# Rests of 64 tokens in 512 B pieces by head pair, measured starts in the plan, and a last store in three parts

## The chip, the cores and the metric

One core of one Trainium2 chip. The metric is the device time of one execution in microseconds (us). All runs that are compared are of the state "fast", and each kernel was timed beside the kernel before on the same chip. A ratio is the mean time of one kernel's fast runs over that of the other's fast runs of the same rounds, so it is not quite the quotient of the medians that are also given. A ratio difference of 0.01 is about 2.5 us.

## The reference, cut to what matters

Two attentions in a row, then a feed-forward layer. With B, H, S, D = 8, 8, 576, 64 and 32 packed queries `p`:

```python
p_packed = sm_attn(p, k, v)                  # 32 x 64 per head
out = sm_attn(q, p_packed, p_packed)         # 576 x 64 per head
x = out.transpose(0, 2, 1, 3).reshape(4608, 512)
h = x @ w_in                                 # 512 x 2048
g = h * (1 / (1 + exp(-beta * h)))
return g @ w_out                             # 2048 x 512
```

All inputs are float32 in device memory: q, k, v are 9.4 MB each, w_in and w_out 4 MB each. The output is 9.4 MB.

## The kernel before: the parts that matter

A small planner inside the kernel simulates the engines with a cost for each task and emits every engine's instructions in the resulting order. Ranks with some 1100 hand-searched offsets decide between tasks that are ready. All loads and stores are issued by SyncE (SP), in that order; an engine never skips a waiting instruction.

S = 576 is 512 tokens that spread over 128 partitions, and a **rest** of 64 tokens. For each of q, k, v and each batch the rest (128 KB) is loaded by two DMAs of 64 partitions; each piece is one token of one head, 256 B:

```python
for g in range(2):
    nc.sync.dma_start(
        t[64 * g : 64 * g + 64, :].rearrange("p (h d) -> p h d", h=4),
        src[b, 4 * g : 4 * g + 4, SM:S, :].rearrange("h p d -> p h d"),
    )
```

When the planner has nothing for the tensor engine (PE) before its own 48 us, it emits a useless matmul, which keeps PE busy:

```python
if e == "PE" and now < WARM_UNTIL:
    self.filler()
    free[e] = now + 0.11
```

The last of the 18 output units is stored by one DMA of 512 KB after its last quarter is ready.

The softmax here doesn't subtract the row's maximum and nothing guards it: scores larger than these inputs give would overflow.

## Time and profile before

| | before |
|---|---|
| time, median of 3 (range) | 252.02 us (251.88 to 252.15) |
| span of the profiled run | 250.0 us |
| PE busy, fillers among its matmuls | 237.0 us, 211 |
| last filler, end of the last matmul | 43.4 us, 245.8 us |
| data moved from 2 to 48 us | 324 GB/s on average |
| granted PE clock | 1.00 throughout |

The prediction shows the page and the chain that these stand on.

### The profile page before, as it was taken

The page shows a single profiled execution, that of the slowest core. Times are in us where ns is not written, and L with a number is a line of the kernel's source. Part 1 is how long each engine was busy: PE and PEld are TensorE (multiplying, and loading weights), DVE is VectorE, ACT ScalarE, POOL GpSimd, SP SyncE. Part 2 cuts the span into 40 slices and gives each one's busy share as a digit, 9 for nine tenths or more (in the row PEclk, how much of TensorE's full clock was granted, in tenths as well). Part 3 has the DMA queues.
Part 4 walks back from the last instruction along what each step waited for, and adds up shares of the span by engine and source line. Part 5 has one row for each costly group of instructions (what it writes and reads, how often), then busy time and mean ns, then how long its engine had stood idle before and what let it go on. Part 6 is the DMA issues. An engine that isn't in the chain of part 4 may idle for free.

```text
span 250.0 us, 6818 instructions
## 1 busy us (share of the span) xinstructions
PE 237.0 (95%) x2852; PEld 191.1 (76%) x2852; DVE 174.1 (70%) x327; ACT 176.6 (71%) x312; POOL 71.0 (28%) x119
## 2 busy tenths in 40 slices
PE   4999879899999999999999999999999999999993
PEld 4997557356657987888688977897889878898882
DVE  7464778689679839953996778836983597546752
ACT  2276357697879896898889867987699868875200
POOL 4044341434660164046205932341360000000000
PEclk9999999999999999999999999999999999999999
DMA  6999999999999999999999699999937020111042
GB/s 187 312 276 328 343 333 368 335 332 228 256 277 219 305 264 198 281 259 291 203 271 263 194 254 244 262 232 292 244 121 178 3 89 3 62 62 47 3 146 106
DMA packets 73486, 54.18 MB, mean 217 GB/s; under 512 B 42080, under 2 KB 66672, under 8 KB 73456
## 3 DMA queue, kind: packets, MB, share of 16 engines
q1 hardware_dynamic: 73456, 53.76, 79.2%
q8 instruction: 22, 0.36, 0.6%
q14 instruction: 8, 0.07, 0.1%
HBM read 37.23 MB, written 9.44 MB: 187 GB/s over the span
## 4 chain that ended last, share of the span: by engine, by line
PE 82%; DMA 9%; DVE 3%; SPq 2%; POOL 1%; issue 1%; ACT 0%; POOLq 0%; DVEq 0%
PE o_ps L294 44%; PE h_ps L294 22%; DMA v<-in_v_dram 5%; DMA w_in<-in_moe_w_in_dram 4%; PE w_ps L294 4%; PE hr_ps L294 3%; PE warm_ps L294 2%; PE s_ps L294 2%; PE z_ps L294 2%; SPq L364 1%; PE pp_ps L294 1%; DVE identr L976 1%; POOL w_in_bf L1104 1%; DVE pT L1026 1%; DVE k_bf L394 0%
## 5 line engine op out<-in xcount | busy, mean ns | idle before, releaser
L748 ACT ACTIVATE g_main<-h_ps 128x512 bf16<-128x512 f32 x128 | 71.1, 595 | 31.3 <-PE h_ps L294 30.8
L294 PE MATMUL h_ps<-A2T,W_bf 128*128 128x256 bf16 x512 | 70.1, 273 | 0.5 <-ACT g_rem L770 0.2
L294 PEld LDWEIGHTS <-W_bf 128*128 128x128 bf16 x768 | 56.3, 98 | 14.5 <-issue 7.2
L294 PEld LDWEIGHTS <-g_main 128*128 128x128 bf16 x512 | 48.7, 98 | 10.9 <-issue 1.7
L709 DVE SCALAR_TENSOR_TENSOR W_bf<-w_ps,rz,beta_bc 128x512 bf16<-128x512 f32 x64 | 44.8, 745 | 7.4 <-PE w_ps L294 7.2
L294 PE MATMUL o_ps<-w_out_bf,g_main 128*128 128x256 bf16 (+1 forms) x288 | 46.6, 296 | 0.7 <-DVE w_out_bf L1120 0.7
L294 PEld LDWEIGHTS <-g_sums 128*128 128x128 bf16 x384 | 36.6, 98 | 5.7 <-issue 0.7
L882 DVE COPY o_sb<-o_ps 128x256 f32<-128x256 f32 x48 | 20.2, 422 | 28.1 <-PE o_ps L294 27.5
L309 ACT ACT_TABLE_LOAD x28 | 35.9, 1283 | 1.2 <-PEq L1200 0.7
L294 PE MATMUL o_ps<-w_mix,g_sums 128*128 128x256 bf16 x256 | 34.6, 273 | 0.0
L394 POOL CAST v_bf<-v 128x512 bf16<-128x512 f32 x26 | 18.1, 736 | 47.7 <-PE o_ps L294 22.5
L294 PE MATMUL o_ps<-w_mix,g_main 128*128 128x256 bf16 x224 | 31.4, 273 | 0.0
L880 DVE TENSOR_TENSOR o_sb<-o_sb,o_ps 128x256 f32<-128x256 f32 x48 | 20.1, 419 | 13.5 <-PE o_ps L294 13.0
L394 POOL CAST q_bf<-q 128x512 bf16<-128x512 f32 x26 | 16.7, 684 | 18.6 <-DMA q<-in_q_dram 13.1
L294 PE MATMUL warm_ps<-identr 128*128 128x128 bf16 x211 | 18.3, 239 | 3.7 <-DVE bones L980 3.7
L394 POOL CAST k_bf<-k 128x512 bf16<-128x512 f32 x26 | 15.4, 634 | 14.0 <-DMA k<-in_k_dram 4.1
L294 PEld LDWEIGHTS <-identr 128*128 128x128 bf16 x211 | 14.9, 109 | 5.1 <-DVE bones L980 3.7
L294 PE MATMUL o_ps<-w_out_bf,g_sums 128*128 128x256 bf16 x128 | 17.3, 273 | 0.0
L294 PE MATMUL w_ps<-w_in_bf,pp 64*32 64x512 bf16 x256 | 13.9, 386 | 1.2 <-DVE pp L584 1.0
L294 PEld LDWEIGHTS <-pp 64*32 64x32 bf16 x384 | 5.6, 88 | 11.8 <-issue 8.2
L651 DVE TENSOR_TENSOR A2T<-E2T,z_ps 128x512 bf16<-128x512 bf16 x16 | 10.8, 682 | 1.6 <-ACT z_ps L646 1.6
L882 ACT COPY o_sb<-o_ps 128x256 f32<-128x256 f32 x16 | 6.0, 373 | 7.9 <-PE o_ps L294 7.6
(91 smaller groups left out, 272.7 us busy)
## 6 DMA issues: line engine op xcount, KB each, us to landing
out_dram<-o_sb SPq DMA_DIRECT2D x16, 512.0 KB, 3.3
k<-in_k_dram SPq DMA_DIRECT2D x7, 1024.0 KB, 6.2
v<-in_v_dram SPq DMA_DIRECT2D x7, 1024.0 KB, 7.2
q<-in_q_dram SPq DMA_DIRECT2D x6, 1024.0 KB, 7.4
w_in<-in_moe_w_in_dram SPq DMA_DIRECT2D x4, 1024.0 KB, 9.8
w_out<-in_moe_w_out_dram SPq DMA_DIRECT2D x4, 1024.0 KB, 8.4
q<-in_q_dram SPq DMA_DIRECT2D x4, 512.0 KB, 8.2
k<-in_k_dram SPq DMA_DIRECT2D x2, 512.0 KB, 7.7
```

Of the source, the lines that this page charges most:

```text
L294: return self.nc.tensor.matmul(out, lhsT, rhs, start=start, stop=stop, tile_position=pos, skip_group_check=True)
L309: self.nc.scalar.preload_act_table_set(SETS[mode])
L364: nc.sync.dma_start(t[64 * g : 64 * g + 64, :].rearrange("p (h d) -> p h d", h=4), src[b, 4 * g : 4 * g + 4, SM:S, :].rearrange("h p d -> ...
L394: self.copy[engine](to[:, j : j + m], of[:, j : j + m])
L651: nc.vector.tensor_tensor(part(st[b, "A2"], i), part(st[b, "E2"], i), sums(i), ALU.mult)
L709: nc.vector.scalar_tensor_tensor(st[b, "W"][:, r, cols], st[b, "w", m][:], st[b, "rz1"][:, r : r + 1], self.beta_bc[:, cols], ALU.mult, AL ...
L748: nc.scalar.activation(st[b, v, "g"][:, :, f, :], st[b, "h", v, f][:].rearrange("p (q n) -> p q n", q=4), AF.Silu)
L880: nc.vector.tensor_tensor(o, o, ps, ALU.add)
L882: self.copy[engine](o, ps)
L976: nc.vector.tensor_copy(self.identr[:], self.ident32[:])
L1026: self.copy[engine](self.pT[h, :, 32 * r : 32 * r + 32].rearrange("p m (a s) -> p m a s", a=2)[..., 8 * i : 8 * i + 8], self.t["p_ps", i][ ...
L1104: self.copy[engine](self.w_in_bf[:, c, cols], self.t["w_in", n][:, c])
```

## The change

Its intent: pieces of 512 B for the rests of the first two batches, since the start of the kernel is bound by loads; a plan with measured durations and the real starts of the engines; a shorter last store. The core of the diff (cut: the new table of offsets, the new order of the first loads, the same layout carried through the products and sums, one constant, `pT`, set on another engine, beta spread in halves):

```diff
+LAST_UNIT = 17
+PAIRED = 2
+COST_US = {"g": 0.597, "h": 0.4376, ...}
+FREE_US = {"PE": 2.2, "ACT": 2.1, "DVE": 3.8, "POOL": 2.0}
-OFFSETS = {0: -15, 1: -1.5, ...}
+OFFSETS = {0: -63.2, 1: -4.8, ...}
 ...
             def rest(x=x, b=b, src=src):
+                if b < PAIRED:
+                    for h in range(2):
+                        nc.sync.dma_start(
+                            t[:, 128 * h : 128 * h + 128],
+                            src[b, h:H:2, SM:S, :].rearrange("c (p u) d -> c p (u d)", u=2),
+                        )
+                    return
 ...
         def exp1_rest():
+            if b < PAIRED:
+                for c in range(NC):
+                    rows = slice(32 * c, 32 * c + 32)
+                    nc.scalar.activation(...)       # four of 32x128 for two of 64x128
+                return
 ...
+        if number == LAST_UNIT:
+            for n, (qs, i) in enumerate((((0, 1), 4), ((3,), 5), ((2,), 6))):
+                self.task(("last", n), "SP", 0.5 * len(qs), lambda qs=qs: self.store_part(unit, qs), [taken[i]], -10)
```

A rest now lies as 4 head pairs x 32 token pairs on the 128 partitions. The two tokens of a pair are neighbours in memory, hence the 512 B.

## The prediction

> **What bounds the kernel now.** I read the page first, then the chain of waits in order of time, then tables by stretch for the first 60 us, then the timeline of the start and of the end.
>
> The page says that the tensor engine is the bound nearly everywhere, and where it is not:
>
> ```profile
> PE   4999879899999999999999999999999999999993
> DMA  6999999999999999999999699999937020111042
> PE 82%; DMA 9%; DVE 3%; SPq 2%; POOL 1%; issue 1%; ACT 0%; POOLq 0%; DVEq 0%
> L294 PE MATMUL warm_ps<-identr 128*128 128x128 bf16 x211 | 18.3, 239 | 3.7 <-DVE bones L980 3.7
> ```
>
> PE is at 9 in every slice from about 56 us to the end of the last but one. The last line warns that a busy PE is not always a useful one: 211 matmuls on `warm_ps` are fillers that the planner emits when PE has nothing to do before its clock of 48 us. Forty-five of them ran in 4.98 us (first lines of the chain below), 0.111 us each, so all take 211 x 0.111 = 23.4 us, the last one at 43.4 us. Of the 250.0 us span, PE does no useful work in these 23.4 us, in 3.7 us before its first instruction and in 4.2 us after its last one. The rest, about 219 us, is matmul work that the change does not shorten. So only three things can be won: fillers, head and tail.
>
> The chain of waits names what the fillers wait for, and what the tail is:
>
> ```profile
> 3.68 4.98 PE warm_ps L294 x45
> ...
> 20.03 11.77 DMA v<-in_v_dram
> ...
> 33.95 10.71 DMA w_in<-in_moe_w_in_dram
> 44.71 1.70 POOL w_in_bf L1104 x2
> ...
> 232.73 13.11 PE o_ps L294 x120
> ```
>
> Two loads, of v for batch 1 and of the third block of w_in, carry 22.5 us of the start. Neither is slow by itself: they stand in a queue. This table has, per stretch, the stretch, busy time of each engine, the granted clock (1.00 throughout), the DMA share and GB/s:
>
> ```profile
> 4.00:10.00 6.00, 6.00 (x58) 5.76 (x57) 3.03 (x10) 0.05 (x1) 0.00 (x0) 1.00 1.06 358
> 10.80:12.00 1.20, 1.20 (x19) 1.20 (x16) 1.20 (x3) 0.58 (x1) 0.00 (x0) 1.00 1.19 175
> 14.40:16.80 2.40, 2.40 (x34) 2.38 (x33) 1.29 (x2) 1.94 (x3) 0.66 (x2) 1.00 0.83 134
> 19.20:21.60 2.40, 2.13 (x53) 1.70 (x52) 1.11 (x3) 0.67 (x2) 0.82 (x1) 1.00 1.09 231
> 22.00:26.00 4.00, 3.74 (x54) 3.21 (x54) 2.56 (x5) 2.70 (x5) 2.34 (x5) 1.00 1.04 390
> 40.00:46.00 6.00, 5.28 (x62) 3.18 (x62) 4.78 (x10) 4.09 (x7) 1.33 (x3) 1.00 1.05 378
> ```
>
> All 16 DMA engines are busy, yet in three stretches they move half of what they otherwise move. Those are the rests: the casts that read them wait until 12.51 us (k, batch 0) and 16.37 us (v, batch 0), at the end of the first two dips. The start is therefore bound by the DMA stream, and the 256 B pieces of the rests are its worst part.
>
> **What the Trainium skill says.** (1) "DMA: Bandwidth & Descriptors", Specifications: transfers need at least 512 B to reach line rate; below that the engine reads, modifies and writes. The trace agrees: 134 to 231 GB/s in the dips, 358 beside them. (2) The same page, "Why small descriptors are slow": each packet has a fixed cost. It agrees here too: 358 GB/s where q, k, v come in 1 KB pieces, 378 to 390 where the weights' 2 KB pieces dominate. (3) The same page, "Why a DMA increments its semaphore by 16 and not by 1", how many engines: the count is the largest number up to 16 that divides the slowest dimension of both access patterns. The loads of before have 64 or 128 there, so 16 engines; the trace of before has no load with a smaller one to test it. (4) The same page, "Anatomy of one DMA", gives a fixed 2.0 us plus bytes over 436 GB/s for a DMA from GpSimd: an estimate of 3.2 us for 512 KB and 2.3 us for 128 KB. These stores come from SyncE, and the page has 3.3 and 2.4:
>
> ```profile
> out_dram<-o_sb SPq DMA_DIRECT2D x16, 512.0 KB, 3.3
> out_dram<-o_sb SPq DMA_DIRECT2D x8, 128.0 KB, 2.4
> ```
>
> **The change part by part.**
>
> *Rests.* Six rests (k, v, q of batches 0 and 1) of 128 KB. What one costs now: the dips lose (358-175) x 1.2 + (358-134) x 2.4 + (358-231) x 2.4 = 220 + 538 + 305 = 1063 KB against the plain rate, 2.97 us at 358 GB/s. They hold four rests (k0, v0, k1, q0 by issue order), so 0.74 us each, plus 0.37 us for the bytes themselves: 1.1 us of stream. With 512 packets over 16 engines, 32 each, that is 34 ns for a 256 B packet. A 1 KB packet takes 1024 B / (358/16 GB/s) = 46 ns, a 2 KB one about 85 ns at 384 GB/s; on that line a 512 B packet would take 26 ns (estimate).
>
> If the new loads use 16 engines: 256 packets, 16 each, 0.42 us: 0.68 us saved per rest, 4.1 us for six. But the source of the new load is a pattern of 4 heads x 32 pairs x 128 elements, and the heads do not merge with the pairs. Its slowest dimension is 4, and by (3) it would go on 4 engines: 64 packets on each of these, 1.7 us where 1.1 us was, so +0.6 us per rest and +3.5 us for six on the four engines that then finish every later bulk load last. The same part can win 4.1 us or lose 3.5 us of stream.
>
> How much of it reaches PE: the two loads of the chain stand behind five and six of the rests, but PE has useful work for about half of the first 44 us. I take 0.7 of the stream: -2.9 us or +2.5 us.
>
> *More work for the rests.* In each of two batches: two score matmuls of 256 columns instead of 128 (+0.12 us), two more for the sums and four more for the packed product (about 0.2 us at the spacing of the 10 sums in 0.39 us), and four exponentials where two stood at 0.27 us, +0.54 us on ACT. In batch 0 the ACT work is solid from the rest's exponential (17.90 us) to the end of the other two (19.57 us) and the packed product follows at once, so these 0.54 us can show; in batch 1 the v load ends later and hides them. All in all +0.4 us.
>
> *Last unit in three stores.* The last store of 512 KB is issued at 246.32 us, after the last take, and ends the program. Three of its quarters have been ready earlier: takes end every 0.87 us before. The last piece becomes 128 KB: 3.3 - 2.4 = 0.9 us saved, provided that the two earlier pieces, issued about 1 and 2 us ahead, do not hold the queue (issue takes 0.34 us).
>
> *The plan.* The scheduler gets measured durations and true starts of the engines, wider start-up spreading of beta, the memset of `pT` on DVE, and a new set of rank offsets. From the ranks in the diff I read that k of batch 0 now goes before q and the first two blocks of w_in stand behind the loads of batch 0. In the stretch where PE is solid nothing can come of it. In the start a better order makes useful work out of fillers; the order of before was searched too, so I take only -1.0 us, a judgement and not a count.
>
> *Sum.* With 16 engines: 252.0 - 2.9 + 0.4 - 0.9 - 1.0 = 247.6 us. With 4 engines and no recovery: 252.0 + 2.5 + 0.4 - 0.9 - 1.0 = 253.0 us.
>
> **The rivals.** *A, cheaper packets on 16 engines, 247.6 us.* For it: the dips are plain, and the scheduler's new cost for a rest (0.55 us for 0.8) says that its writer counts on a gain. Against: the slowest dimension. *B, four engines, but they catch up, about 250.5 us.* A single slice of the stream reaches 408 GB/s, 25.5 GB/s per engine against 22.4 in the 1 KB stretch; with twelve engines ahead of them the four may run at that, and then most of the +3.5 us is made up, and the plan and tail remain. *C, four engines that never catch up, 253.0 us:* if each engine's own rate is the limit, as the 46 and 85 ns suggest, every bulk load until the end of the start lands later and fillers or waits grow. *D, the rests are hidden anyway:* the gain is only plan and tail, 252.0 - 0.9 - 1.0 + 0.4 = 250.5 us, the same number as B by another road. A later bound (ACT 71%, DVE 70%) is unlikely to take over, as neither's share moves by more than half a per cent.
>
> **Range and chances.** I give A 45%, B and D together 35%, C 20%: 0.45 x 247.6 + 0.35 x 250.5 + 0.2 x 253.0 = 249.7, say 249.6 us. The range runs from a little under A to C: 246.8 to 252.8 us. Faster by over 2% means under 247.0 us, which needs A and a plan that gives more than I take: 16%. Slower by over 2% means above 257 us, beyond C: 3%. The rest, 81%, is within 2%.
>
> **What would show it.** Packets: six rests save 256 each (1536), the last store adds 256, so about 72,200 in place of 73,486, and about 39,000 under 512 B. The rate in the dips: gone under A; under B and C stretches with a low DMA share, as twelve engines stand idle, and rests that land later than 8 us after issue. Fillers: about 180 of 211 under A, as many or more under C. Tail: the end 3.3 us after the last matmul instead of 4.2 us. The stretch from the last filler to the last matmul should keep its length within 1 us of 202 us; if it grows, the error is in my claim that the change leaves the solid part alone. The prediction is wrong in kind if the start shrinks without a faster stream: then it is the order of loads that did it, which I put at 1 us.

## The result, and the profile after

| | before | after |
|---|---|---|
| time, median of 4 (range) | 251.95 us (251.82 to 252.15) | 261.06 us (259.33 to 261.93) |
| ratio, 95% interval | | 1.0352 (1.0294 to 1.041) |
| span of the profiled run | 250.0 us | 260.1 us |
| fillers, last filler | 211, 43.4 us | 173, 59.8 us |
| end of the last matmul to the end | 4.2 us | 3.4 us |

The change made the kernel 3.5% slower, outside the range of the prediction. The rows of the changed kernel's page that answer to those of before (slices of 6.5 us; the third row is the granted PE clock in tenths):

```profile
PE   6867788689899999999999999999999999999994
PEclk9997889679999999999999999999999999999999
DMA  6989989989979899999999999979994210012033
PE 75%; DMA 10%; SPq 7%; DVE 4%; issue 1%; ACT 0%; POOL 0%; POOLq 0%
DMA packets 72094, 54.18 MB, mean 208 GB/s; under 512 B 38896, under 2 KB 65280, under 8 KB 72064
```

The loss is all at the start. From the twelfth slice on PE is at 9 as before. In the first eleven it has holes, its clock falls, and the DMA engines, which were busy all the time before, are not. SyncE's queue, 2% of the chain before, is 7%. The packets are close to the prediction (72,094 for 72,206 and 38,896 for 39,008), so the 512 B pieces are there. That both are 112 short will matter in experiment 10.

The same stretches in the table by stretch, columns as in the prediction. First the kernel before:

```profile
2.00:48.00 46.00, 39.90 (x551) 32.10 (x552) 30.36 (x63) 23.42 (x44) 15.18 (x21) 1.00 1.06 324
12.00:20.00 8.00, 7.48 (x121) 6.99 (x121) 4.55 (x8) 5.89 (x10) 2.58 (x2) 1.00 1.03 279
48.00:60.00 12.00, 11.55 (x118) 6.75 (x116) 10.89 (x20) 10.30 (x19) 3.61 (x7) 1.00 1.04 301
```

and the changed kernel:

```profile
2.00:48.00 46.00, 36.58 (x491) 30.37 (x493) 25.57 (x55) 22.60 (x43) 10.08 (x17) 0.93 0.95 287
12.00:20.00 8.00, 4.75 (x78) 4.04 (x76) 3.75 (x8) 4.34 (x10) 0.40 (x1) 1.00 0.82 223
48.00:60.00 12.00, 10.14 (x53) 4.16 (x53) 6.00 (x13) 5.64 (x12) 5.88 (x8) 0.72 0.95 321
```

From 12 to 20 us only 223 GB/s move, with a DMA share of 0.82: engines stand idle. PE is busy for 4.75 of these 8 us instead of 7.48. Later, from 48 to 60 us, its clock is 0.72.

The chain of waits of the changed kernel names the loads:

```profile
9.13 7.58 DMA q32r<-in_q_dram
17.25 0.65 SPq L376
17.95 8.02 DMA k32r<-in_k_dram
...
36.38 11.45 DMA w_out<-in_moe_w_out_dram
47.86 1.29 DVE w_out_bf L1182 x3
```

Two of the small rests (`q32r`, `k32r`; a DMA of 64 KB) take 7.6 and 8.0 us from issue to landing and hold up what comes after them. In the kernel before, no rest was among the long pieces of this chain; the long loads there had 1 MB. The 7.6 and 8.0 us alone say little: before, the rests of the first 62 us took 6.0 to 8.2 us in the median, since they too stood in a queue. What is new is SyncE. It issues in a fixed order, and the issues themselves got longer. The two issues of the rest of v, batch 0, in the changed kernel and in the kernel of experiment 9, which has the same plan:

```profile
11.99 2.68 SPq L376 DMA_DIRECT2D v32r<-in_v_dram  x2
8.90 1.36 SPq L376 DMA_DIRECT2D v32r<-in_v_dram  x2
```

From 4 to 42 us SyncE spends 36.5 us inside its issues in the changed kernel and 26.3 us in that of experiment 9, for 25 issues begun in each (28.8 us for 24 in the kernel before; sums over the trace). From 11.99 to 19.27 us it gets out two rests and one load of 1 MB, for which it takes 4.8 us in experiment 9 (8.90 to 13.70 us); the next loads aren't issued yet while engines stand idle. Why an issue takes longer isn't shown; a backlog on a few engines would fit, though the short one of experiment 5 left the issues at 0.5 us.

**Theories.** Theory 1: the source pattern of a paired rest has 4 as its slowest dimension, so each of these 12 DMAs runs on 4 of 16 DMA engines; every later load needs these 4 too and ends when they do. Theory 2: the new order of loads and tasks is at fault. Theory 3: the paired layout costs time on ACT and PE (twice as many exponentials, more matmuls).

### The profile page after: what moved, and what is told of

The parts are those of the page before. It is cut to its first block, busy times and chain, and to the rows that moved or that the text cites. A ratio compares the mean times of both kernels' runs of the same rounds, so it can differ in the third digit from the quotient of the medians.

```text
span 260.1 us, 6770 instructions
## 1 busy us (share of the span) xinstructions
PE 241.2 (93%) x2821; PEld 191.2 (74%) x2826; DVE 175.9 (68%) x328; ACT 177.8 (68%) x316; POOL 70.6 (27%) x118
## 2 busy tenths in 40 slices
DMA packets 72094, 54.18 MB, mean 208 GB/s; under 512 B 38896, under 2 KB 65280, under 8 KB 72064
## 4 chain that ended last, share of the span: by engine, by line
PE 75%; DMA 10%; SPq 7%; DVE 4%; issue 1%; ACT 0%; POOL 0%; POOLq 0%
PE o_ps L303 44%; PE h_ps L303 19%; DMA w_out<-in_moe_w_out_dram 4%; PE w_ps L303 3%; SPq L367 3%; SPq L376 3%; DMA k32r<-in_k_dram 3%; DMA q32r<-in_q_dram 3%; PE hr_ps L303 3%; DVE w_out_bf L1182 2%; PE z_ps L303 2%; PE s_ps L303 2%; DVE W_bf L752 2%; PE pp_ps L303 1%; SPq L1151 0%
## 5 line engine op out<-in xcount | busy, mean ns | idle before, releaser
L303 PE MATMUL o_ps<-w_out_bf,g_main 128*128 128x256 bf16 (+1 forms) x283 | 47.7, 304 | 3.2 <-DVE w_out_bf L1182 2.2
L303 PE MATMUL o_ps<-w_mix,g_main 128*128 128x256 bf16 x224 | 30.5, 272 | 0.3 <-DVE o_sb L925 0.3
L412 POOL CAST v_bf<-v 128x512 bf16<-128x512 f32 x26 | 16.2, 666 | 36.7 <-DMA v<-in_v_dram 27.0
L412 POOL CAST q_bf<-q 128x512 bf16<-128x512 f32 x26 | 17.8, 724 | 21.6 <-issue 11.8
L412 POOL CAST k_bf<-k 128x512 bf16<-128x512 f32 x26 | 17.6, 720 | 12.8 <-DMA k<-in_k_dram 7.7
L303 PE MATMUL warm_ps<-identr 128*128 128x128 bf16 x173 | 17.4, 248 | 2.4 <-DVE bones L1041 2.4
L303 PEld LDWEIGHTS <-identr 128*128 128x128 bf16 x173 | 13.3, 113 | 4.3 <-DVE bones L1041 2.4
L661 ACT ACTIVATE E2T<-s_ps,rz 128x512 bf16<-128x512 f32 x16 | 10.1, 684 | 7.7 <-PE s_ps L303 7.6
## 6 DMA issues: line engine op xcount, KB each, us to landing
w_out<-in_moe_w_out_dram SPq DMA_DIRECT2D x4, 1024.0 KB, 11.5
```

The source lines that it names most:

```text
L303: return self.nc.tensor.matmul(out, lhsT, rhs, start=start, stop=stop, tile_position=pos, skip_group_check=True)
L412: self.copy[engine](to[:, j : j + m], of[:, j : j + m])
L661: nc.scalar.activation(st[b, "E2"][:, i, 0:SM], st[b, "s2", i][:], AF.Exp, scale=st[b, "rz1"][:, i : i + 1])
```

## The experiments

### 1. The new plan with 16 engines, four DMAs per rest

```diff
-for h in range(2):
-    nc.sync.dma_start(t[:, 128 * h : 128 * h + 128],
-        src[b, h:H:2, SM:S, :].rearrange("c (p u) d -> c p (u d)", u=2))
+for c in range(NC):
+    nc.sync.dma_start(t[32 * c : 32 * c + 32, :].rearrange("p (h e) -> p h e", h=2),
+        src[b, 2 * c : 2 * c + 2, SM:S, :].rearrange("h (p u) d -> p h (u d)", u=2))
```

> The changed kernel, but each paired rest is loaded by four DMAs (one per 32 partitions, both heads of a pair side by side), so that the slowest dimension of both patterns is 32 and 16 engines can share it; same 512 B pieces, same plan, same instructions on all other engines. Theory 1 (the rests run on 4 engines and everything behind them queues): back to 247 to 251 us, no stretch at a DMA share near 0.7 in the first 40 us, granted clock 1.0. Theory 2 (the new order of loads and tasks is to blame): stays at 259 to 262 us. Theory 3 (the paired layout's extra work on ACT and PE is to blame): stays at 259 to 262 us.

Measured: 254.58 us (254.16 to 255.16), ratio 1.0075 (1.0036 to 1.0113). Some 7 us of the loss are gone (1.0352 - 1.0075) with the instructions on PE the same, row for row. That speaks for theory 1 and against 2 and 3 as the main cause. It isn't the 247 to 251 us that I expected: this form is still slower than before, its clock was 0.978 to 0.993 and not 1.0, and its DMA share still fell, to 0.45 from 16 to 18 us.

### 2. The new plan with the rests of before

```diff
-PAIRED = 2
+PAIRED = 0          # and the planner still told the costs of the paired form
```

> The new plan and the three last stores, but the rests as before (256 B pieces, two DMAs of 64 partitions, two slots of scores fewer); the planner is still told the costs of the paired form, so the order of tasks is that of the changed kernel. Theory 1: 249 to 253 us, as before's rests use 16 engines. Theory 2: 258 to 262 us. Theory 3: 249 to 253 us.

Measured: 253.56 us (251.99 to 254.59), ratio 1.0025 (0.9963 to 1.0088), half a microsecond over the 249 to 253 us that theories 1 and 3 expect and far from theory 2's 258 to 262 us. Theory 2 falls as the main cause. The new plan together with the new last store still gives nothing here.

### 3 and 4. The old plan with paired rests, on 4 and on 16 engines

Only the paired rests (and the layout that they need) are put into the kernel before; the plan's order is kept. Number 3 loads them as the change does, number 4 with the four DMAs of experiment 1.

> The kernel before, plan and last store kept, with the paired rests exactly as the change loads them (two DMAs, 4 heads as the slowest dimension of the source). Theory 1: 256 to 262 us. Theory 2: 251 to 253 us. Theory 3: 256 to 262 us.

> The kernel before with paired rests, each by four DMAs of 32 partitions on 16 engines. Theory 1: 249 to 252 us, a little under before since 512 B pieces are cheaper. Theory 2: 251 to 253 us. Theory 3: 256 to 262 us.

Measured: number 3 took 258.72 us (257.33 to 259.93), ratio 1.0235 (1.0182 to 1.0288); number 4 took 254.14 us (253.22 to 254.69), ratio 1.0052 (1.001 to 1.0094). The rests alone, in the plan of before, cost 2.4%, and three quarters of it go away with another shape of DMA that moves the same bytes in the same pieces to the same places. Theory 3 falls as the main cause. But number 4 missed its 249 to 252 us too: cheaper pieces brought nothing in this form.

### 5. The forms side by side, in the quiet end

A probe was added to the kernel before: after 203 us, when only stores use the DMA engines, three rests are loaded in each of four forms. The probe ran once (state unknown); only its trace is used.

```diff
+A: two DMAs, as before                  t[64g:64g+64] <- "h p d -> p h d"
+B: two DMAs, as the change              t[:, 128h:]   <- "c (p u) d -> c p (u d)"
+C: four DMAs of 32 partitions           t[32c:32c+32] <- "h (p u) d -> p h (u d)"
+D: two DMAs, token pair slow            t[:, 128h:]   <- "c (p u) d -> p c (u d)"
```

> The kernel before with a probe in its quiet end (after about 200 us, when only stores use the DMA engines): three 128 KB rests in each of four forms, one form after the other, each waiting until the one before has been read. A: as before (64 partitions, 256 B pieces, 2 DMAs). B: as the change (128 partitions, 512 B pieces, source with 4 heads slowest, 2 DMAs). C: four DMAs of 32 partitions, 512 B pieces. D: the same source as B with the token pairs slowest (32) and 128 partitions, 2 DMAs. If B runs on 4 engines, its stretch shows a DMA share near 0.25 and takes about 4 x 1.7 = 5 us or more for 384 KB where D has a share near 1 and takes about 1.3 us plus 2 us of latency. If B used 16 engines, B and D would look alike. C tells whether 32 partitions limit the engines too: like D if not, like B or half way if so.

SyncE's issues in the probe (start, total time, number):

```profile
206.99 1.27 SPq L1171 DMA_DIRECT2D formA<-in_q_dram  x2
221.19 1.10 SPq L1177 DMA_DIRECT2D formB<-in_q_dram  x2
230.33 1.78 SPq L1183 DMA_DIRECT2D formC<-in_q_dram  x4
234.91 1.18 SPq L1189 DMA_DIRECT2D formD<-in_q_dram  x2
```

and the last of the three casts that wait for each form:

```profile
210.32 0.82 POOL L1200 CAST probe<-formA 128x256 bf16<-128x256 f32 x1 [0.23 <-DMA formA<-in_q_dram]
226.38 0.60 POOL L1200 CAST probe<-formB 128x256 bf16<-128x256 f32 x1 [0.93 <-DMA formB<-in_q_dram]
233.99 0.40 POOL L1200 CAST probe<-formC 128x256 bf16<-128x256 f32 x1 [1.80 <-DMA formC<-in_q_dram]
237.96 0.40 POOL L1200 CAST probe<-formD 128x256 bf16<-128x256 f32 x1 [1.05 <-DMA formD<-in_q_dram]
```

From the end of the last issue to the start of the cast that needs it: A 2.1 us (210.32 - 208.26), C 1.9 us, D 1.9 us, but B 4.1 us (226.38 - 222.29). B alone leaves a backlog. While SyncE had nothing more of B to issue:

```profile
222.40:224.60 2.20, 2.20 (x38) 2.03 (x37) 0.44 (x3) 1.68 (x3) 0.40 (x1) 1.00 0.27 76
```

A share of 0.27 of 16 engines is 4.3 engines. The trace doesn't name the engines, but it counts them in another way: a DMA leaves packets of 4 B besides its data. From 220.8 to 224.6 us, with B's DMAs alone at work, and from 234.8 to 238.1 us, with D's:

```profile
DMA packets 590, 0.29 MB, mean 77 GB/s; under 512 B 16, under 2 KB 590, under 8 KB 590
DMA packets 577, 0.28 MB, mean 84 GB/s; under 512 B 64, under 2 KB 576, under 8 KB 576
```

B's 574 packets of 512 B are 4.5 DMAs of 128, with 16 small packets: about four a DMA. D's 512 are four DMAs, with 64: sixteen a DMA. If each engine that takes part leaves one, B ran on 4 engines and D on 16. With four, 76 GB/s are 19 GB/s each, or 27 ns for a 512 B packet, which is also the median duration of these packets in the trace; the prediction had estimated 26 ns. B's 768 packets ran from 220.5 to 225.7 us, 5.1 us (the expectation's "4 x 1.7 = 5 us" should read 3 x 1.7).

My expectation for D, a share near 1, was a miss, and so the shares of the other forms say nothing of their engine counts: outside B it is the issue that limits the rate. Away from the stores, a DMA of 64 KB takes SyncE 0.53 to 0.67 us, one of 32 KB in form C 0.35 to 0.44 us. So form C costs 1.78 us of issue per rest where A, B and D cost 1.1 to 1.3 us.

That experiments 1 and 4 missed has a larger companion in SyncE's waits of the first 62 us. Apart from one long wait for w_in (5.5 to 6.6 us) that all three have, SyncE waited 11.5 us in number 1 and 12.1 us in number 4 for earlier DMAs to land before it issued the next one, and 1.2 us in the kernel before. Why four DMAs a rest bring such waits isn't shown. A hole in one place is no evidence for the issue time: from 20 to 24 us the share is 0.54 in number 4, but 0.55 in number 3, which has two DMAs a rest. I didn't separate this from the paired layout's own cost by an experiment of four DMAs alone.

### 6. The last store alone

```diff
-self.plan_store(unit, taken)
+if number == LAST_UNIT: ...three stores, as in the change; the kernel before otherwise
```

> The kernel before with the last unit's store in three pieces and nothing else. Theory: the last piece is 128 KB instead of 512 KB, and 0.9 us is saved (ratio 0.9964). Rival: the three issues queue behind each other and nothing is saved (ratio 1.000).

Measured: 251.67 us (251.21 to 252.39) in six runs, ratio 0.9963 (0.9929 to 0.9998). The predicted 0.9 us is there.

### 7. Fillers in the waits of the changed kernel

```diff
+if b == 0: self.fill(12)        # ahead of the packed product; five more such places,
                                 # each just before an instruction that waited for a load; 65 in all
```

> The changed kernel with 65 more useless matmuls, placed right before the six places where PE stood still for a load in the first 50 us, so that they run in the waits (they delay nothing unless a wait is shorter than I placed matmuls for). If the lower granted clock (0.5 to 0.9 of full between 20 and 56 us) adds to the loss, the clock rises above 0.99 and the time falls by 2 to 4 us, to 257 to 259 us. If the clock is only a sign of waiting for data, the time stays at 260 to 262 us.

Measured: 259.13 us (258.88 to 259.34), ratio 1.0253 (1.0216 to 1.029), mean clock 0.993 instead of 0.973. So 65 more useless matmuls make the changed kernel about 2.5 us faster (1.0352 - 1.0253; 0.8 to 4.2 us with both intervals). In the changed kernel from 20 to 24 and from 48 to 56 us:

```profile
20.00:24.00 4.00, 2.79 (x39) 2.15 (x40) 0.84 (x2) 0.06 (x1) 0.80 (x2) 0.60 0.88 242
48.00:56.00 8.00, 6.42 (x24) 2.16 (x24) 5.34 (x11) 3.21 (x7) 3.58 (x4) 0.57 0.91 296
```

From 48 to 56 us, 24 matmuls fill 6.42 us at a clock of 0.57; this is the first work on w_out, which had to wait for its load. The Trainium skill describes the gate ("TensorE: Matmul & The Clock Gate", Part 1): an idle window of about 3.4 us lets the clock fall to half. The trace agrees in kind: after PE was busy for 1.07 of the 4 us from 18 us on, single stretches of 2 us show 0.50. But no gap between PE's matmuls is longer than 1.95 us there, so PE need not stand still for the whole window. The clock is a second cost of late data. It isn't the main one.

### 8 and 9. The same pieces on 16 engines without more issues

If theory 1 holds, it is enough to put the 32 token pairs, not the 4 head pairs, in the slowest place. The partition of a piece becomes 4p + c instead of 32c + p. Rows of one head pair then are no longer neighbours, so the exponential can't be cut by rows; a matmul of 4 rows adds -800 to the scores outside a row's head pair, and one exponential of 128x512 does for four.

```diff
-src[b, h:H:2, SM:S, :].rearrange("c (p u) d -> c p (u d)", u=2)
+src[b, h:H:2, SM:S, :].rearrange("c (p u) d -> p c (u d)", u=2)
 ...
+self.mm(ps[:, 256 * u : 256 * u + 256], self.pick[0:4, :], self.off[0:4, :], start=False)
 ...
-for c in range(NC): nc.scalar.activation(...32 rows...)
+nc.scalar.activation(E()[:, 4:6, :], ..., AF.Exp, scale=SCALE)
 ...
-return st[b, "q", "Tr"][h, :, 32 * c : 32 * c + 32].rearrange("d u p -> d p u")
+return st[b, "q", "Tr"][h, :, c:128:NC].rearrange("d u p -> d p u")
```

Number 8 is this in the old plan with the three last stores, number 9 in the changed kernel.

> The kernel before with its plan, the three last stores, and paired rests in another order of partitions (token pair slow, head pair fast), so that the same two DMAs per rest have 32 as the slowest dimension of the source and 128 of the tile: 16 engines, 512 B pieces, no more issues than before. The mask between head pairs is added on PE by a matmul of 4 rows, so that one exponential of 128x512 stands for the four of the change. Theory (512 B pieces on 16 engines shorten the stream by about 0.5 us a rest, and PE gets most of it): 249 to 250.5 us, ratio 0.988 to 0.993. Rival (the start is held by what SyncE waits for before it issues the next loads and by the issue time of each DMA, which does not change): only the last store is saved, ratio about 0.996.

> The changed kernel with its plan and the rests of the run above. Theory (the change is sound but for the 4 engines, and the extra issues of the four-DMA form cost the rest): 247 to 250 us. Rival (the new order of loads and tasks gives nothing or costs on the chip whatever the rests do): 252 to 254 us, as with the old rests or with four DMAs.

Measured: number 8 took 249.64 us (249.02 to 251.28), ratio 0.9884 (0.9858 to 0.991); number 9 took 249.19 us (248.98 to 249.66), ratio 0.9866 (0.9846 to 0.9885). Both theories' numbers came in, and both rivals fell. These two kernels beat the kernel before and the changed one, and both give the right result. Number 9 in the stretches of before, and the chain's long loads in it:

```profile
2.00:48.00 46.00, 42.02 (x548) 32.24 (x550) 31.57 (x70) 27.18 (x49) 15.96 (x25) 1.00 1.06 354
12.00:20.00 8.00, 7.90 (x145) 6.54 (x143) 4.00 (x9) 5.31 (x9) 1.12 (x3) 1.00 1.09 347
48.00:60.00 12.00, 11.26 (x119) 7.27 (x119) 11.58 (x19) 9.51 (x18) 4.46 (x5) 1.00 1.12 289
```

```profile
16.86 11.65 DMA v<-in_v_dram
28.53 9.32 DMA w_out<-in_moe_w_out_dram
37.88 1.29 DVE w_out_bf L1192 x3
```

The dip from 12 to 20 us is gone: 347 GB/s where the changed kernel had 223. The first use of w_out begins at 37.88 us instead of 47.86 us. The clock is 1.00 again, with the same 173 fillers.

### 10. The same kernel, back on 4 engines

Number 9 also has another mask. To see that the mask is not what helps, this run keeps it and puts the head pairs in the slowest place again:

```diff
-src[b, h:H:2, SM:S, :].rearrange("c (p u) d -> p c (u d)", u=2)
+src[b, h:H:2, SM:S, :].rearrange("c (p u) d -> c p (u d)", u=2)     # and one constant and one read to match
```

> The faster kernel with the changed plan (mask by a matmul, one exponential), with nothing else altered but the order of partitions in the rests, back to that of the change: head pair slow, so the source's slowest dimension is 4 again. It differs from the faster kernel in the patterns of 12 loads, of one constant and of one read of the transposed q. If the 4 engines are the cause, 258 to 261 us. If the mask and the single exponential had made the difference, 249 to 252 us.

Measured: 260.46 us (258.99 to 262.24), ratio 1.0334 (1.0267 to 1.0402). This is the changed kernel's time again:

```profile
2.00:48.00 46.00, 37.77 (x496) 30.98 (x497) 25.88 (x58) 21.76 (x37) 10.05 (x17) 0.89 0.96 285
12.00:20.00 8.00, 4.94 (x78) 4.21 (x78) 3.94 (x8) 3.59 (x6) 0.40 (x1) 0.99 0.85 223
```

The order of two letters in the pattern of 12 loads costs 1.0334 - 0.9866, which is 4.7% or 11.8 us of 252. The packet counts say the same as the probe: number 9 has 72,238 packets (39,040 under 512 B) and number 10 has 72,094 (38,896), so 144 small ones are missing, 12 for each of the 12 loads, as for 4 engines in place of 16. The changed kernel's 112 too few are these 144 less 32 for the two additional stores.

## Why the prediction was wrong, by its own steps

The runs give a sum, each term as a difference of two ratios times 252 us (it closes by construction, as each term begins where another ends):

| term | from | us | predicted |
|---|---|---|---|
| last store in three | 0.9963 | -0.9 | -0.9 |
| 512 B pieces on 16 engines, with their layout | 0.9884 - 0.9963 | -2.0 | -2.9 + 0.4 |
| new plan | 0.9866 - 0.9884 | -0.5 | -1.0 |
| 4 engines in place of 16 | 1.0334 - 0.9866 | +11.8 | +5.4 (C less A) |
| four exponentials in place of the mask | 1.0352 - 1.0334 | +0.5 | (in the 0.4) |
| sum | 1.0352 - 1 | +8.9 | |

The new plan's and the exponentials' terms are smaller than the intervals of the runs that they come from. The terms also depend on the order in which they are taken. In the plan of before, paired rests on 4 engines (number 3, less 0.0037 for the last store) against 16 (number 8) cost 1.0198 - 0.9884, 7.9 us with the exponentials, and not 11.8 + 0.5. So the new plan gains a little when the loads come in time and makes late loads dearer.

**What held.** The start is bound by the DMA stream; the tail is 0.9 us; a 512 B packet takes about 26 ns (27 in the trace). The engine count read from the pattern was right as well: a head count of 4 in the slowest place does confine the load. Branch A (247.6 us) is 1.6 us from what the kernel with 16 engines took, but in part by luck. The prediction gave all that the three dips lost to the rests, which made a 256 B packet 34 ns. In the trace of the kernel before, these packets take 23.4 ns on average (median 18) in the first 62 us; the 512 B packets of number 9 take 27.8 ns. By this a rest saves 32 x 23.4 - 16 x 27.8 ns = 0.3 us, 1.8 us for six and not 4.1, and about all of it reached the end and not 0.7. The dip from 14.4 to 16.8 us shows what else was in it: SyncE issued nothing from 10.60 to 14.40 us, and in number 8, with cheap rests, 14 to 16 us still moves only 94 GB/s at a share of 0.42. One reading was also off by one: the load of v on the chain stands behind four rests (k0, v0, k1, q0), not five.

**The step that failed** is the size of the 4-engine term. The prediction put it at "+3.5 us for six on the four engines", took "0.7 of the stream", and so had +2.5 us for branch C, 5.4 us above A. The runs show 11.8 us between the two, for three reasons.

First, the loads were later than the stream's own loss. Per rest, 64 packets instead of 16 on each of the four engines at 27 ns are 1.3 us, so 7.8 us for six against branch A; the prediction's 4.1 + 3.5 = 7.6 us agrees with that. But the first use of w_out slipped by 10.0 us (47.86 - 37.88). The prediction let only "the four engines" lag; it did not have SyncE, whose issues took 10 us more between 4 and 42 us, while engines ran dry. Nor were its packets at 27 ns: in the trace of the changed kernel the 512 B packets of the start take 38 ns on average, and 28 in number 9, which would make it 64 x 38 - 16 x 28 ns = 2.0 us a rest, 12 us for six. Late data can also cause waits in its turn, as loads wait for buffers that are freed by work on earlier data. No run separates what makes up the extra 2 us.

Second, the reasoning behind the factor 0.7 was wrong: I took it that PE has useful work for half of the start and so hides part of a delay. But PE runs its instructions in a fixed order, and fillers are fixed too. A load that is late stops PE outright. More than the whole slip of w_out reached the end (11.8 us of 10.0), the loss of the clock included.

Third, a stopped PE is then clocked down. Experiment 7 puts this at about 2.5 us in the changed kernel. The prediction had no such term.

**The rivals.** B, that the four engines catch up, fell. The changed kernel moved 287 x 46 us = 13.2 MB from 2 to 48 us. Less the rests (0.79 MB) each engine's share is 0.78 MB, and the four carried a quarter of the rests, 0.20 MB, on top: 0.97 MB in 46 us, 21 GB/s. With all 16 sharing (number 9) each engine moved 354/16 = 22 GB/s. On average the four were no faster with idle engines beside them (how long the four themselves stood still isn't known; in the probe's backlog they made 19). D, that the rests are hidden anyway, fell with experiment 8. C was the right branch. It had 20%, while A had 45%, on the ground that the planner's cost for a rest shows that its writer counts on a gain. A cost in a plan is a hope and not a measurement; the only evidence on the engine count spoke for 4.

**Signs that were badly chosen.** "Fillers: about 180 of 211 under A, as many or more under C": the count is 173 in both, since it is fixed at build time. The sign to look for is the time of the last filler (47.8 us in number 9, 59.8 us in the changed kernel) and the granted clock. Two more signs were no better. The stretch from the last filler to the last matmul, said to keep 202 us within 1, is 196.9 us in the changed kernel but 196.1 us in number 9 too: the new plan moved the fillers. And a rest that lands later than 8 us after its issue is no sign of B or C: in the kernel before, one took 11.5 us.

## What to carry to other kernels

Before a load is reshaped for larger pieces, look at the slowest dimension of both its patterns: with 4 there, the loads here ran on a quarter of the DMA engines, and everything queued behind them waited. Here another order of the tile put 32 first, and the mask and the strided read that it needed cost far less than the 11.8 us. Where a plan fixes each engine's order, a late load can stop the tensor engine for its full delay and lower its clock on top, so don't discount it by the share of useful work.

## What the Trainium skill lacked or had wrong

- "DMA: Bandwidth & Descriptors", the section on why a DMA increments its semaphore by 16, has the rule for the number of engines, and it held (about 4 small packets a DMA in form B and 16 in form D; a share of 0.27 for form B, 4.1 us from issue to use where the other forms had 1.9 to 2.1). What it lacks is what this does to the loads behind: SyncE spent 36.5 us instead of 26.3 us inside its issues from 4 to 42 us, the stream fell from 347 to 223 GB/s from 12 to 20 us, and 12 small loads (0.79 MB of 54 MB) cost 11.8 us.
- The same page, Specifications, gives 512 B as the least size for line rate. In the probe's backlog 512 B pieces moved at 19 GB/s per engine (76 GB/s over four, the four being inferred), against 22.4 GB/s for 1 KB pieces (358/16), so 512 B is better than 256 B but some 15% short. The median durations of packets in the probe's trace say the same: 18 ns for 256 B, 27 for 512 B, 46 for 1 KB, 88 for 2 KB and 159 for 4 KB, which fits about 9 ns plus the bytes at 27 GB/s (an estimate from these five).
- I found no page that gives SyncE's issue time by the number of pieces in a DMA. Here it was 0.61 us for 256 pieces (form A), 0.53 to 0.67 us for 128 (B and D), and 0.43 us for 64 (C). Outside the backlog this, and not the engines, set the rate of small loads in the probe.
- "TensorE: Matmul & The Clock Gate", Part 1, has the gate right in kind. It doesn't say how much work an idle window may hold: here the clock fell to 0.5 with no gap between PE's matmuls longer than 1.95 us, and 65 useless matmuls won back about 2.5 us of 261.
